# One core: the first loads and the order of every instruction found anew in a planned attention and channel-mix kernel

## The chip, the cores and the metric

The kernel runs on one core of one Trainium2 chip. The metric is the time of one execution on the device in microseconds (us), lower is better. The engines have these names in the profile: PE is TensorE's matmul, PEld its weight load, DVE is VectorE, ACT is ScalarE, POOL is GpSimd, SP is SyncE, which issues all the DMAs here.

## What is computed

Attention with rotary embeddings over 8 batches, 8 heads, 576 tokens and 64 dimensions a head; its output, 512 wide, goes through a gated channel mix with a hidden width of 1024. Everything is float32.

```
def _attn_ref(q, k, v):
    ...
    q_rot, k_rot = (rotate(q), rotate(k))
    scale = 1.0 / np.sqrt(D)
    scores = scale * np.matmul(q_rot, k_rot.transpose(0, 1, 3, 2))
    scores = scores - np.max(scores, axis=-1, keepdims=True)
    attn = np.exp(scores)
    attn = attn / (np.sum(attn, axis=-1, keepdims=True) + 1e-09)
    return np.matmul(attn, v).astype(np.float32)

def _moe_ref(x, mu_k, mu_r, w_k, w_v, w_r):
    ...
    xk = mu_k * x + (1.0 - mu_k) * x_prev
    xr = mu_r * x + (1.0 - mu_r) * x_prev
    k = np.maximum(xk @ w_k, 0.0)
    v = k * k @ w_v
    r = 1.0 / (1.0 + np.exp(-(xr @ w_r)))
    return (r * v).astype(np.float32)
```

## The kernel before

**Attention.** Two heads of a batch make a pair, and there are 32 pairs. For each pair `plan_rope` (L369) loads keys and queries with their swapped halves beside them (`xk`, `xq`, from one ring of two buffers, `nat`), multiplies both by the table of cosines and sines `turn`, and adds the two products. The first nine pairs (`PLAIN`) use the sum as it is (`kh`, `qh`); for the later ones it is split in a high and a low half (`kh`, `kl`, `qh`, `ql`), and the scores are made of three products. `plan_unit` (L429) makes the scores of 128 query rows: the products (L445), on VectorE the maximum (L454), on ScalarE the exponentials (L458), on VectorE the transposition of 32 x 32 blocks (L461). `plan_values` (L495) multiplies by the values in three parts (L520), and `plan_total` (L541) divides by the sums into `xT`.

**Channel mix.** `plan_mix` (L585) makes xk and xr of half a batch (288 tokens) and splits them (`mxh`, `mxl`). `plan_product` (L616) makes each product with the weights out of three (L625, L626, L627): high by high, low by high, high by low. `plan_key` (L635) makes relu, square and split (`kkh`, `kkl`), `plan_gate` (L666) the sigmoid, `plan_value` (L679) the product of both and the store.

**Weights.** They come in as raw 64-bit words, 20 blocks of 512 KB: 8 of w_k, 4 of w_r, 8 of w_v. `plan_convert` (L332) loads a block into a buffer of the ring `ql` (two buffers), decodes it with three steps on ScalarE (L345, L351) and two sums on VectorE or GpSimd (`wm`), casts it to the high half (L312 on ScalarE, L314 on VectorE) and subtracts for the low half.

**What sets the order.** No engine's order is written out. Each step is given to `Plan.op` with a rank, a list of what it needs, the buffers it uses and, for each engine that may do it, a duration and a bias. `Plan.issue` (L120) then plays the kernel through: an engine that becomes free takes, of the steps that are ready, the one with the lowest rank plus bias. The order so found is the order of the instructions of each engine. `one` and `two` (L294, L298) give a step to ScalarE or VectorE, and to GpSimd or VectorE; `B_SPLIT` is VectorE's bias for casts, `B_ROPE` for rotary steps, `B_LOW` for low halves. `lead` (L75) adds to a rank what `R` has for the kind of step and, for the first six pairs, what `EARLY` has. The rank of a pair is 18 times its number plus `PB`, that of a batch's channel mix 72 times its number plus `m0` and `MB`; a block of weights has a rank along `wk0` to `wk1` (or `wr`, `wv`) plus its entry in `WORDS`, and its load the same less 3. The load of keys and queries adds `ld`. All these numbers came out of a search. GpSimd and VectorE are played as taking turns for the steps marked with True (`port`), weighted by `WAIT`.

Of the kernel before, what the change touches and what calls it, by code (L numbers as in the profile page):

```python
# [25 lines left out]
R = dict(sg=146.09, k=35.07, q=51.6, v=-92.97, cs=-1440.03, ld=485.93, rope0=775.97, rope1=1341.24, rope2=-1593.82,
         split0=-490.14, split1=1651.45, u0=-9.23, u1=-9.99, u2=4.09, u3=-0.28, u4=-4.95, mx=-547.8, ex=-53.52,
         rz=-72.52, rs=-791.65, dg=-117.58, bd=451.61, tr=-238.29, ev=349.84, av=17.88, av2=630.69, tot=-1148.65,
         bor=-1152.78, m0=203.43, mh=-3.64, mk=10.46, mr=30.95, ms=1.47, tp=1238.89, rc=-454.17, mx1=-529.45,
         mx2=-1335.32, mx3=704.87, mg=3.37, mv=-0.23, dr=-1079.44, key0=1189.23, key1=-720.87, key2=14.38,  # L30
         gate0=-847.6, gate1=481.76, wk0=-48.7, wk1=233.61, wr0=-724.28, wr1=-1281.69, wv0=-20.84, wv1=1945.66)
# [4 lines left out]
EARLY = dict(k=(-1008.01, -482.85, -254.73, -397.74, 52.63, -212.54), q=(-618.65, -612.78, -339.46, -240.87, -281.62,  # L36
             23.47), v=(-438.31, -468.46, -152.53, -193.2, -99.8, -96.79), u0=(-1879.98, -368.38, -203.28, -241.45,
             75.91, 24.41), u1=(-217.97, -1062.91, -434.13, -122.46, 5.8, 24.25), u2=(-1055.68, -331.48, -170.26,
             -150.99, -114.87, 10.87), u3=(-1096.85, -646.9, -220.35, -256.66, -144.42, 32.2), u4=(-452.73, -641.08,
             -406.66, -274.78, 47.37, 35.29), mx=(-353.68, -484.47, -458.2, -302.05, -156.39, -150.07), ex=(-349.96,  # L40
             -41.28, -1342.06, 392.41, 2389.5, 993.44), tp=(-233.86, -2103.85, 654.43, -485.72, 608.35, 775.94),
             rs=(-93.75, 199.83, -142.38, -154.85, -142.68, -36.14), av=(14.66, -44.42, -95.87, -127.56, 58.88, 37.7),
             av2=(6.64, -352.36, -379.73, 83.33, -1292.92, 167.87), rc=(-1169.1, -848.81, -888.54, -532.26, -674.54,
             -118.59), tot=(-382.56, -430.1, -195.11, -8.86, -95.78, -89.47), rope0=(-853.79, -396.42, 1771.49, 997.6,
             520.07, -291.51), rope1=(-465.54, 808.19, -805.76, -1024.78, 647.78, -966.37), rope2=(-148.08, -152.31,
             -462.39, 3.34, -218.25, -248.75))
# [10 lines left out]


def act(n):
    return 0.833 * n + 100  # L60


def dve(n):
# [195 lines left out]
def rope_attention_channel_mix(ctx, tc, qt, kt, v, cs, mu, w_k, w_v, w_r, out):  # L259
# [4 lines left out]
    B, NP, _, _, S = kt.shape  # L264
# [38 lines left out]
    V, A, G, T = nc.vector, nc.scalar, nc.gpsimd, nc.tensor  # L303
# [28 lines left out]
    def plan_convert(t, src, hi, lo):  # L332
        d = {}
        s_w, s_e, s_m = Slot("ql"), Slot("kl"), Slot("wm")

        def load():
            words = sb.tile([P, 513, 2], U32, tag="ql", name="raw", bufs=BUFS["ql"])
            quarters = words.rearrange("p n w -> p (n w)").bitcast(I16)
            nc.sync.dma_start(quarters[:, 1:2049], src)
            d["middle"] = words[:, 0:512, 1]  # L340
            d["top"] = quarters.rearrange("p (n w) -> p n w", w=4)[:, 1:513, 0]

        def signed(n, tag, scale):
# [4 lines left out]
        e = op("A", t, act(512) + 130, lambda: signed("e", "kl", 1.0), [o], [s_w, s_e])  # L348
        m = op("A", t, act(512) + 130, lambda: signed("m", "wm", -1.0), [o], [s_w, s_m])
        m = op(two(512, B_LOW), t, 0, lambda e: combine(e, d["m"], d["e"], d["m"], ALU.subtract), [e, m], [s_m, s_e])  # L350
        e = op("A", t, act(512) + 80, lambda: A.mul(d["e"], d["middle"], 2.0 ** -13), [m], [s_w, s_e])  # L351
# [77 lines left out]
    def plan_unit(t, d, c):  # L429
# [17 lines left out]
        m = op("T", t, (8 if d["plain"] else 6) * (120 + 12), products, (d["q"][:c + 1] if d["plain"] else d["q"]) + d["k"], slots + d["sq"] + d["sk"], ("row" if c < 4 else "full", (8 if d["plain"] else 12) * len(heads)))  # L447
        for x in heads:
            s_m = Slot("nm")
            place = c + 5 * x  # L450
# [44 lines left out]
    def plan_values(t, d):  # L495
# [45 lines left out]
    def plan_total(t, d, half, w, slots, o, apart):  # L541
# [251 lines left out]
```

## Time and profile before

| | |
|---|---|
| median of 3 executions | 977.1 us (976.92 to 977.46) |
| the profiled execution | 977.65 us |
| its span, first to last instruction | 975.8 us |
| busy, share of the span | TensorE 94%, VectorE 79%, ScalarE 58%, GpSimd 54% |
| TensorE's mean granted clock | 0.983 |
| read from HBM, written | 88.74 MB, 9.44 MB |

The page of the profile gives each engine's busy time and count of instructions, then the span in 40 slices with a digit for the busy tenths of each. Matmuls are pipelined: a record is longer than the step from one to the next, and a TensorE that is shown as busy all the time may still have small gaps. A wait is put down to the last thing that released it.

### The profile page before, as it was taken

Reading aid. Unit: us, or ns where it says so; the run is one execution under the profiler, and the core shown is the slowest. Engines: PE = TensorE matmul, PEld = TensorE weight load, DVE = VectorE, ACT = ScalarE, POOL = GpSimd, SP = SyncE. Lnnn points to the kernel's source line nnn. Section 1 sums busy time; section 2 is a strip of 40 time slices with the busy share of each in tenths; the row PEclk is TensorE's granted clock in tenths of the full one; section 3 lists DMA queues with packets and bytes.
Section 4 is the critical chain, followed back from the end, with each engine's and each line's share of the span. In section 5 each row is a group of like instructions: output and inputs, shape, how many; then the busy total and the mean of one; then the engine's idle time right before and its main releaser. Section 6 shows DMA issues by size and latency. Waiting matters only on the chain.

```text
span 975.8 us, 34418 instructions
## 1 busy us (share of the span) xinstructions
PE 920.2 (94%) x15134; PEld 814.8 (83%) x15134; DVE 775.3 (79%) x1255; ACT 568.1 (58%) x1394; POOL 525.0 (54%) x551
## 2 busy tenths in 40 slices
PE   1888799999999999999999999999999999999998
PEld 1456588888989988899889998899888998989998
DVE  5999997986879878696896968797886969876552
ACT  4767885464747565474765747375664747544243
POOL 6988793543746556273753656474662647221201
PEclk9968899999999999999999999999999999999999
DMA  7455603422222333222233333033332232111000
GB/s 285 133 198 201 220 30 117 160 108 81 91 71 108 115 113 108 71 101 98 81 113 115 108 108 103 32 108 114 114 108 94 89 108 82 42 61 57 19 25 26
DMA packets 30854, 100.38 MB, mean 103 GB/s; under 512 B 3056, under 2 KB 11504, under 8 KB 26608
## 3 DMA queue, kind: packets, MB, share of 16 engines
q1 hardware_dynamic: 30704, 98.19, 28.8%
q8 instruction: 118, 1.93, 0.8%
q14 instruction: 32, 0.26, 0.1%
HBM read 88.74 MB, written 9.44 MB: 101 GB/s over the span
## 4 chain that ended last, share of the span: by engine, by line
PE 74%; DVE 18%; ACT 3%; DMA 2%; issue 2%; POOL 1%; SPq 0%; DVEq 0%; ACTq 0%
PE acc L625 18%; PE av L520 15%; PE acc L626 14%; PE acc L627 14%; PE s L445 12%; DVE nm L454 5%; DVE p L461 4%; DVE mxf L600 3%; DVE xk L308 2%; ACT p L458 2%; DMA xq<-in_qt 1%; DMA xk<-in_kt 1%; DVE rt L681 1%; PE av L526 1%; DVE xq L308 1%
## 5 line engine op out<-in xcount | busy, mean ns | idle before, releaser
L458 ACT ACTIVATE p<-s,nm 128x576 f32<-128x576 f32 x288 | 212.0, 740 | 99.6 <-DVE nm L454 98.5
L454 DVE TENSOR_REDUCE nm<-s 128x1 f32<-128x576 f32 x288 | 202.7, 737 | 13.4 <-PE s L445 12.9
L461 DVE STREAM_TRANSPOSE p<-p 128x576 f32<-128x576 f32 x288 | 206.7, 750 | 4.7 <-ACT p L458 4.6
L445 PE MATMUL s<-kh,qh 64*128 64x288 f32 (+1 forms) x738 | 143.8, 424 | 41.1 <-POOL qh L308 17.7
L520 PE MATMUL av<-p,values 32*64 32x144 f32 x9216 | 177.6, 293 | 2.7 <-issue 2.4
L520 PEld LDWEIGHTS av<-p,values 32*64 32x64 f32 x9216 | 150.9, 134 | 22.5 <-issue 19.4
L625 PE MATMUL acc<-mxh,wk_h 128*128 128x288 f32 x512 | 160.9, 314 | 3.4 <-ACT hr L642 3.2
L625 PE MATMUL acc<-kkh,wv_h 128*128 128x288 f32 x512 | 158.3, 309 | 4.5 <-DVE rt L681 4.3
L445 PEld LDWEIGHTS s<-kh,qh 64*128 64x128 f32 (+1 forms) x738 | 79.8, 204 | 88.6 <-ACT p L458 29.0
L626 PE MATMUL acc<-kkl,wv_h 128*128 128x288 f32 x512 | 151.1, 295 | 0.0
L626 PE MATMUL acc<-mxl,wk_h 128*128 128x288 f32 x512 | 150.8, 295 | 0.0
L627 PE MATMUL acc<-kkh,wv_l 128*128 128x288 f32 x512 | 150.8, 295 | 0.0
L627 PE MATMUL acc<-mxh,wk_l 128*128 128x288 f32 x512 | 150.6, 294 | 0.0
L308 POOL TENSOR_TENSOR kkl<-hr,kkh 128x288 fp32r<-128x288 f32 x97 | 88.1, 917 | 59.0 <-ACT kkh L312 42.1
L625 PEld LDWEIGHTS acc<-mxh,wk_h 128*128 128x128 f32 x512 | 96.1, 188 | 21.7 <-issue 14.1
L625 PEld LDWEIGHTS acc<-kkh,wv_h 128*128 128x128 f32 x512 | 96.1, 188 | 18.1 <-issue 11.1
L564 POOL COPY last<-xT 128x1 f32<-128x1 f32 x32 | 6.3, 196 | 190.3 <-DVE xT L557 190.3
L308 POOL TENSOR_TENSOR mxl<-mxf,mxh 128x288 fp32r<-128x288 f32 x77 | 69.7, 913 | 72.4 <-DVE mxh L314 49.4
L681 DVE TENSOR_TENSOR rt<-acc,rt 128x288 f32<-128x288 f32 x64 | 28.8, 449 | 95.3 <-PE acc L627 94.0
L548 ACT COPY rp<-av 128x288 f32<-128x288 f32 (+1 forms) x68 | 22.8, 389 | 135.3 <-PE av L526 134.8
L600 DVE SCALAR_TENSOR_TENSOR mxf<-xT,mu_t,mxf 128x288 f32<-128x288 f32 x128 | 95.6, 755 | 6.2 <-ACT mxf L595 5.2
L626 PEld LDWEIGHTS acc<-mxl,wk_h 128*128 128x128 f32 x512 | 96.3, 188 | 0.1
(85 smaller groups left out, 1945.2 us busy)
## 6 DMA issues: line engine op xcount, KB each, us to landing
values<-in_v SPq DMA_DIRECT2D x32, 1152.0 KB, 5.5
xq<-in_qt SPq DMA_DIRECT2D x31, 640.0 KB, 5.0
xk<-in_kt SPq DMA_DIRECT2D x32, 576.0 KB, 4.2
out_dram<-rt SPq DMA_DIRECT2D x64, 144.0 KB, 1.7
raw<-in_w_v SPq DMA_DIRECT2D x8, 512.0 KB, 4.1
raw<-in_w_k SPq DMA_DIRECT2D x8, 512.0 KB, 3.8
raw<-in_w_r SPq DMA_DIRECT2D x4, 512.0 KB, 5.5
turn<-in_cs SPq DMA_DIRECT2D x1, 640.0 KB, 4.9
```

Source lines behind the costliest of these rows:

```text
L308: (V if e == "V" else G).tensor_tensor(out=out, in0=a, in1=b, op=op)
L445: T.matmul(w[x][:, h, 0:H], lhsT=kind(d[q][r, c * P:(c + 1) * P]), rhs=kind(d[k][r, h * H:(h + 1) * H]), start=i == 0, stop=i == len(todo) ...
L454: V.tensor_reduce(out=w["nm", x], in_=w[x][:, :, 0:H], op=ALU.max, axis=AX.XY, negate=True)
L458: A.activation(out, w[x][:, :, 0:H].rearrange("p a (b n) -> p a b n", n=32), AF.Exp, bias=w["nm", x], scale=1.0, accum_out=d["sums"][:, pl ...
L461: V.transpose(queries(d, place), queries(d, place))
L520: T.matmul(at(a, x, 0), lhsT=d["vf"][g, b * P + x * D:b * P + x * D + D], rhs=d["pt"][g, b, x * Q:x * Q + Q], start=b == 0, stop=b == NB - 1)
L548: A.copy(w["r", half][:, i], r[..., 256:256 + N // 2])
L600: V.scalar_tensor_tensor(out=x["f"], in0=d["x", half][:, 1:1 + n], scalar=mu_t[:, m:m + 1], in1=x["f"], op0=ALU.mult, op1=ALU.add)
L625: T.matmul(w["a"], lhsT=w_h[:, i, sl], rhs=x["h"], start=(i == 0), stop=False)
L626: T.matmul(w["a"], lhsT=w_h[:, i, sl], rhs=x["l"], start=False, stop=False)
L627: T.matmul(w["a"], lhsT=w_l[:, i, sl], rhs=x["h"], start=False, stop=(i == count - 1))
L681: o = op("V", t + R["dr"], dve(n), lambda: V.tensor_tensor(out=x["r"], in0=w["a"], in1=x["r"], op=ALU.mult), [done, o], [s_a, s_r])
```

## The change

No step is added or taken away. The ranks (`R`, `PB`, `MB`, `EARLY`, `WORDS`), the biases and `WAIT` get other numbers, and eight durations that the planner plays with are set anew: a ScalarE step without its columns from 100 to 66 ns, the decoding steps, the exponentials (140 to 185 on top, so 720 to 731 ns in all), a unit of scores of plain pairs from 1056 to 936 and of later ones from 792 to 750, a block of the attention-value products from 268 to 245, the copy of the sums. By the new ranks the angles, the first keys and the first queries are asked for ahead of the first weights.

```
-R = dict(sg=146.09, k=35.07, q=51.6, v=-92.97, cs=-1440.03, ld=485.93, rope0=775.97, rope1=1341.24, rope2=-1593.82,
...
-         gate0=-847.6, gate1=481.76, wk0=-48.7, wk1=233.61, wr0=-724.28, wr1=-1281.69, wv0=-20.84, wv1=1945.66)
-PB = (-723.84, -349.44, -190.24, -77.24, -72.02, -34.42, -6.06, -3.63)
-B_COPY, B_ROPE, B_SPLIT, B_LOW, B_MIX, B_SQUARE, B_RELU, B_SMALL = 24.24, -108.4, -210.6, 1965.84, 1592.71, -340.79, 2795.13, 87.32
-MB = (-62.06, 30.2, 205.85, 245.13, 245.82, 267.52, 302.28, 1004.59)
+R = dict(sg=114.24, k=26.54, q=27.71, v=-165.25, cs=-2128.35, ld=527.56, rope0=639.18, rope1=1511.2, rope2=-2064.32,
...
+         gate0=-398.63, gate1=366.09, wk0=15.07, wk1=-105.67, wr0=-443.36, wr1=-1370.78, wv0=-8.87, wv1=1784.1)
+PB = (-668.25, -361.66, -199.7, -89.98, -84.16, -58.67, 7.84, 5.25)
+B_COPY, B_ROPE, B_SPLIT, B_LOW, B_MIX, B_SQUARE, B_RELU, B_SMALL = 24.24, 113.23, 75.44, 2514.79, 1178.12, -496.85, 2589.9, 87.32
+MB = (-48.78, 118.24, 163.28, 162.65, 217.96, 323.39, 533.17, 526.21)
...
-EARLY = dict(k=(-1008.01, -482.85, -254.73, -397.74, 52.63, -212.54), q=(-618.65, -612.78, -339.46, -240.87, -281.62,
...
+EARLY = dict(k=(-1894.6, -528.24, -282.01, -420.76, 120.85, -66.18), q=(-1780.54, -995.11, -351.98, -408.07, -163.76,
...
-WORDS = dict(wk=(-121.4, 190.81, -484.21, -187.48, -676.5, -230.26, -396.88, -48.1), wr=(-669.08, -168.07, -568.72,
-             -12.23), wv=(-1028.61, 127.34, -751.85, -1078.14, -297.95, -786.25, 273.13, -765.83))
+WORDS = dict(wk=(171.55, 485.05, -674.03, -560.38, -722.88, -154.92, -495.69, -447.27), wr=(14.78, -531.48, -610.94,
+             -55.56), wv=(-996.99, 319.78, -760.84, -1080.91, -32.96, -990.38, -21.43, -806.77))
...
-WAIT = 1.297e+06
+WAIT = 2.292e+04
...
 def act(n):
-    return 0.833 * n + 100
+    return 0.833 * n + 66
...
-        m = op("T", t, (8 if d["plain"] else 6) * (120 + 12), products, ...
+        m = op("T", t, ((936 if d["plain"] else 750) if c < 4 else (8 if d["plain"] else 6) * 132), products, ...
...
-            o = op("A", t + lead("ex", d["pi"]) + 0.1 * x, act(S) + 140, exponentials, [o], [slots[x], s_m, d["sp"], d["ss"]])
+            o = op("A", t + lead("ex", d["pi"]) + 0.1 * x, act(S) + 185, exponentials, [o], [slots[x], s_m, d["sp"], d["ss"]])
...
-            o = op("T", t + (i * lead("av2", d["pi"])), 2 * n * 134 + 2 * 134 * last, lambda i=i: part(i), ...
+            o = op("T", t + (i * lead("av2", d["pi"])), n * 245 + 244 * last, lambda i=i: part(i), ...
```

## Rows read from the trace of the kernel before

**Rows 1.** Three stretches: length; busy us and records of PE, PEld, DVE, ACT, POOL; clock, DMA.

```profile
0.00:10.40 10.40, 0.00 (x0) 0.00 (x0) 0.83 (x3) 5.96 (x8) 2.18 (x10) 1.00 0.83 293
10.40:117.60 107.20, 78.64 (x1384) 53.43 (x1384) 103.66 (x138) 74.01 (x158) 93.61 (x79) 0.84 0.57 201
117.60:972.60 855.00, 841.58 (x13751) 761.33 (x13750) 670.31 (x1114) 488.17 (x1230) 429.22 (x462) 1.00 0.26 88
```

**Rows 2.** Timeline of SyncE: start us, us, the load that it issues.

```profile
0.72 0.39 SPq L339 DMA_DIRECT2D raw<-in_w_r  x1
1.17 0.42 SPq L706 DMA_DIRECT2D turn<-in_cs  x1
...
2.58 0.65 SPq L378 DMA_DIRECT2D xk<-in_kt  x1
```

**Rows 3.** Timeline of the other engines at the start, idle time and releaser in brackets.

```profile
4.56 0.75 ACT L345 ACTIVATE we<-raw,below 128x512 int32<-128x512 int16 x1 [2.56 <-DMA raw<-in_w_r]
...
5.97 0.69 DVE L308 TENSOR_TENSOR wm<-we,wm 128x512 int32<-128x512 int32 x1 [5.13 <-ACT wm L345]
6.08 1.27 ACT L709 ACTIVATE turn<-turn 128x1280 f32<-128x1280 f32 x1
...
10.52 1.98 DVE L308 TENSOR_TENSOR xk<-xk,turn 128x576 f32<-128x576 f32 x1 [3.77 <-DMA xk<-in_kt]
...
17.75 3.24 PE L445 MATMUL s<-kh,qh 64*128 64x288 f32 x10 [17.75 <-POOL qh L308]
```

**Rows 4.** Loads, KB each, median us to landing: all key loads, then the angles.

```profile
xk<-in_kt SPq DMA_DIRECT2D x32, 576.0 KB, 4.2
...
turn<-in_cs SPq DMA_DIRECT2D x1, 640.0 KB, 4.9
```

**Rows 5.** By tile: ns min/median/max, first and last start in us.

```profile
L625 PE MATMUL acc<-mxh,wk_h x512: 289/295/509, 117.7 to 953.0; 128*128 128x288 f32 x171
...
L308 POOL TENSOR_TENSOR wv_l<-wm,wv_h x7: 1262/1299/1793, 35.0 to 144.6; 128x512 fp32r<-128x512 f32 x7
...
L625 PE MATMUL acc<-kkh,wv_h x512: 289/294/509, 150.2 to 972.0; 128*128 128x288 f32 x171
```

**Rows 6.** VectorE's groups from 10.4 to 117.6 us: busy us, mean ns, idle before.

```profile
L308 DVE TENSOR_TENSOR xk<-xk,turn 128x576 f32<-128x576 f32 x9 | 13.6, 1516 | 3.8 <-DMA xk<-in_kt 3.8
L308 DVE TENSOR_TENSOR xq<-xq,turn 128x640 f32<-128x640 f32 (+2 forms) x8 | 11.5, 1447 | 0.0
...
L314 DVE CAST wk_h<-wm 128x512 fp32r<-128x512 f32 x2 | 1.7, 835 | 0.2 <-POOL xT L562 0.2
...
L314 DVE CAST wr_h<-wm 128x512 fp32r<-128x512 f32 x1 | 1.4, 1399 | 0.0
L314 DVE CAST wv_h<-wm 128x512 fp32r<-128x512 f32 x1 | 1.3, 1274 | 0.0
```

**Rows 7.** By tile xk, whole span: ns min/median/max, first and last start.

```profile
L308 POOL TENSOR_TENSOR xk<-xk,turn x41: 1399/1430/1958, 10.5 to 813.1; 128x576 f32<-128x576 f32 x41
...
L308 DVE TENSOR_TENSOR xk<-xk,turn x23: 705/1131/1979, 10.5 to 815.1; 128x576 f32<-128x576 f32 x23
```

**Rows 8.** TensorE's waits from 250 to 880 us: total us, times, longest.

```profile
PE s L445 <- ACT p L458: 4.7, 6, 1.2
PE acc L625 <- DVE rt L681: 3.8, 4, 1.0
PE acc L625 <- ACT hr L642: 3.0, 5, 0.6
```

**Rows 9.** Chain that ended last, near 380 us: start us, us, what.

```profile
378.56 1.78 POOL ql L308
...
380.36 4.50 DMA xq<-in_qt
```

**Rows 10.** The same chain, an attention-value part; then its group on the page.

```profile
311.14 1.71 PE av L520 x96
...
L520 PE MATMUL av<-p,values 32*64 32x144 f32 x9216 | 177.6, 293 | 2.7 <-issue 2.4
```

More of the change, by code (lines that the diff above doesn't have):

```diff
@@ L25 @@
 PLAIN = 9
-R = dict(sg=146.09, k=35.07, q=51.6, v=-92.97, cs=-1440.03, ld=485.93, rope0=775.97, rope1=1341.24, rope2=-1593.82,
[L27 to L30, printed above, removed]
-         gate0=-847.6, gate1=481.76, wk0=-48.7, wk1=233.61, wr0=-724.28, wr1=-1281.69, wv0=-20.84, wv1=1945.66)
@@ L47 @@
-WORDS = dict(wk=(-121.4, 190.81, -484.21, -187.48, -676.5, -230.26, -396.88, -48.1), wr=(-669.08, -168.07, -568.72,
-             -12.23), wv=(-1028.61, 127.34, -751.85, -1078.14, -297.95, -786.25, 273.13, -765.83))
+R = dict(sg=114.24, k=26.54, q=27.71, v=-165.25, cs=-2128.35, ld=527.56, rope0=639.18, rope1=1511.2, rope2=-2064.32,
+         split0=-418.07, split1=1608.34, u0=-8.2, u1=-5.32, u2=1.49, u3=-6.02, u4=-0.73, mx=-544.32, ex=41.97,
+         rz=-695.55, rs=-754.16, dg=-117.58, bd=451.61, tr=-238.29, ev=349.84, av=13.51, av2=784.94, tot=-1475.95,
+         bor=-1328.95, m0=291.99, mh=-0.32, mk=-23.68, mr=-5.73, ms=2.69, tp=1071.62, rc=-270.84, mx1=-892.1,
+         mx2=-1659.22, mx3=643.01, mg=3.82, mv=0.3, dr=-1319.74, key0=1331.92, key1=-528.48, key2=397.69,
+         gate0=-398.63, gate1=366.09, wk0=15.07, wk1=-105.67, wr0=-443.36, wr1=-1370.78, wv0=-8.87, wv1=1784.1)
@@ new lines @@
+PB = (-668.25, -361.66, -199.7, -89.98, -84.16, -58.67, 7.84, 5.25)
+B_COPY, B_ROPE, B_SPLIT, B_LOW, B_MIX, B_SQUARE, B_RELU, B_SMALL = 24.24, 113.23, 75.44, 2514.79, 1178.12, -496.85, 2589.9, 87.32
+MB = (-48.78, 118.24, 163.28, 162.65, 217.96, 323.39, 533.17, 526.21)
+NE = 6
+EARLY = dict(k=(-1894.6, -528.24, -282.01, -420.76, 120.85, -66.18), q=(-1780.54, -995.11, -351.98, -408.07, -163.76,
+             20.68), v=(-313.84, -466.2, -566.04, -215.27, -126.88, 68.8), u0=(-2315.28, -271.51, -448.14, -301.33,
+             -109.73, -63.6), u1=(-386.55, -870.03, -323.12, -142.79, -62.19, 14.61), u2=(-875.18, -508.09, -196.7,
+             -230.87, -55.43, -50.21), u3=(-1377.19, -764.16, -201.77, -112.33, -132.29, -25.44), u4=(-531.2, -525.98,
+             -407.08, -247.46, -52.6, -80.53), mx=(-632.72, -629.35, -442.49, -448.34, -385.52, -228.35), ex=(-610.02,
+             111.8, -1480.22, 597.82, 2474.47, 797.93), tp=(362.2, -2650.19, 484.55, -96.23, 633.48, 504.81),
+             rs=(133.33, -184.35, -175.83, -175.58, -65.69, 59.18), av=(-148.5, -76.89, -113.79, -116.09, 35.62,
+             5.99), av2=(250.66, -554.68, -325.83, 446.76, -1656.68, -132.39), rc=(-1009.01, -644.13, -615.36,
+             -628.04, -651.4, -278.2), tot=(-887.51, -629.27, -171.89, -250.51, -148.73, -127.64), rope0=(-739.43,
+             -550.11, 1901.03, 1063.51, 499.47, -78.05), rope1=(-896.71, 188.81, -210.14, -1415.44, 601.97, -980.71),
+             rope2=(-134.4, -231.6, 131.18, 273.47, -60.6, -101.5))
@@ L347, in plan_convert @@
         o = dma(t - 3, P * 4096, load, [], [s_w])
-        e = op("A", t, act(512) + 130, lambda: signed("e", "kl", 1.0), [o], [s_w, s_e])
-        m = op("A", t, act(512) + 130, lambda: signed("m", "wm", -1.0), [o], [s_w, s_m])
+        e = op("A", t, act(512) + 99, lambda: signed("e", "kl", 1.0), [o], [s_w, s_e])
+        m = op("A", t, act(512) + 99, lambda: signed("m", "wm", -1.0), [o], [s_w, s_m])
         m = op(two(512, B_LOW), t, 0, lambda e: combine(e, d["m"], d["e"], d["m"], ALU.subtract), [e, m], [s_m, s_e])
-        e = op("A", t, act(512) + 80, lambda: A.mul(d["e"], d["middle"], 2.0 ** -13), [m], [s_w, s_e])
+        e = op("A", t, act(512) + 11, lambda: A.mul(d["e"], d["middle"], 2.0 ** -13), [m], [s_w, s_e])
         m = op("G", t, pool(512), lambda: combine("G", d["m"], d["m"], d["e"], ALU.add), [m, e], [s_m, s_e])
@@ L445, in products @@
                         T.matmul(w[x][:, h, 0:H], lhsT=kind(d[q][r, c * P:(c + 1) * P]), rhs=kind(d[k][r, h * H:(h + 1) * H]), start=i == 0, stop=i == len(todo) - 1)
-        m = op("T", t, (8 if d["plain"] else 6) * (120 + 12), products, (d["q"][:c + 1] if d["plain"] else d["q"]) + d["k"], slots + d["sq"] + d["sk"], ("row" if c < 4 else "full", (8 if d["plain"] else 12) * len(heads)))
+        m = op("T", t, ((936 if d["plain"] else 750) if c < 4 else (8 if d["plain"] else 6) * 132), products, (d["q"][:c + 1] if d["plain"] else d["q"]) + d["k"], slots + d["sq"] + d["sk"], ("row" if c < 4 else "full", (8 if d["plain"] else 12) * len(heads)))
         for x in heads:
@@ L535, in plan_values @@
             need = need + [d["R"]] if last else need
-            o = op("T", t + (i * lead("av2", d["pi"])), 2 * n * 134 + 2 * 134 * last, lambda i=i: part(i), need, slots + [d["sp"], d["sv"]] + [d["srw"]] * last, ("row", 32 * (n + last)))
+            o = op("T", t + (i * lead("av2", d["pi"])), n * 245 + 244 * last, lambda i=i: part(i), need, slots + [d["sp"], d["sv"]] + [d["srw"]] * last, ("row", 32 * (n + last)))
             need = [o]
@@ L566, in border @@
                 G.tensor_copy(xT[:, 0:1], d["last"])
-        o = op("A", t + lead("rc", d["pi"]) + 0.1 * half, act(288) + 60 + 160 * apart, copied, [o], slots + [s_r])
+        o = op("A", t + lead("rc", d["pi"]) + 0.1 * half, act(288) + 160 * apart, copied, [o], slots + [s_r])
         o = op("V", t + lead("tot", d["pi"]) + 0.1 * half, dve(288) + 30 + 130 * apart, total, [o], slots + [s_r, sx])
```

10 lines of the change are left out of this document (removed).

## Prediction

> **What bounds the kernel now.** I read the page first: TensorE is busy for 94% of the span and VectorE for 79%, but TensorE's slices differ between the first few and the rest, so these are averages over stages. I cut the span where the first feed-forward product starts, at 117.7 us [rows 5], and where the first key lands, and asked for the busy time in three stretches [rows 1]. Until 10.4 us the loads set the pace: TensorE does nothing, VectorE is busy for 0.83 us. From 10.4 to 117.6 us VectorE is busy for 103.66 of 107.2 us (97%), GpSimd for 93.61, ScalarE for 74.01; TensorE is granted a clock of 0.84 on average and still waits, so its half-speed stretches cost nothing there. From 117.6 to 972.6 us TensorE is busy for 841.58 of 855 us. So the time is three pieces added up: a start of 10.4 us that waits for data, a prologue of 107 us set by VectorE and by what it shares with GpSimd, and 855 us set by TensorE. The last 3.2 us (975.8 − 972.6) are the last store.
>
> **The sum's base.** The profiled execution took 977.65 us, 1.85 us more than its span of 975.8, and 0.55 us (0.06%) more than the median of 977.1. A gain read in the trace I take off the median.
>
> **Part 1: the first loads.** No instruction is added or taken away; the planner's ranks change, and with them every engine's order. The ranks of the first loads can be added up by hand. Before: the third block of w_r has −724.28 − 278.70 − 568.72 − 3 = −1574.7, the angles −1440.0, the first block of w_r −1396.4, the first keys −723.84 + 35.07 − 1008.01 + 485.93 = −1210.9, the first queries −805.0. That is the order of SyncE in the trace: raw at 0.72 us, turn at 1.17, then mu and a second raw, xk at 2.58 [rows 2]. After: angles −2128.4, keys −668.25 + 26.54 − 1894.6 + 527.56 = −2008.8, queries −1893.5 and −1779.3, and only then w_r with −443.36 − 463.71 − 610.94 − 3 = −1521.0. All of them go through SyncE's one queue; what moves back in it are two blocks of w_r, and whoever waits for those moves back too: ScalarE's first decoding step, and behind it GpSimd's first sum.
>
> What it is worth: VectorE's first rotary multiplication starts at 10.52 us, after 3.77 us of waiting for the keys [rows 3]. The keys are the fifth load issued, and 512 + 640 + 4 + 512 KB stand ahead of them. Afterwards only 640 + 4 KB do. The nearest row is the angles' own in the kernel before: second in the queue behind 512 KB, issued at 1.17 us, landed 4.9 us later, at 6.1 us [rows 2, 4]. The keys would be issued at about 1.6 us; with 4.2 us to landing (the median of all key loads, [rows 4]) they are there at 5.8 us, with 4.9 us at 6.5 us. ScalarE's scaling of the angles (1.27 us, [rows 3]) ends by then if the angles land at about 4.7 us as the first raw block did (ScalarE took it up at 4.56 us, [rows 3]). I take 6.5 us, 4.0 us earlier than 10.52. But VectorE had already done 0.69 us of weight work in that time [rows 3], and GpSimd at most the 2.18 us for which it was busy at all [rows 1]; this must now be done later. VectorE's net is 3.3 us, GpSimd's 1.8 or more. **I take −3.0 us**, nearer to VectorE's, which is the fuller, between −4.7 (5.8 us, nothing moved behind) and 0 (the first rival). The first product, at 17.75 us before [rows 3], should move further, to 11 to 13 us: from the first rotary step it took 7.2 us (17.75 − 10.52), in which GpSimd's weight steps stood between the rotary steps. That further gain counts for nothing, since TensorE waits for VectorE through the whole prologue.
>
> **Part 2: who does the shared steps.** An operation that several engines can do is taken by the engine that first reaches it; a bias makes VectorE take it later. For casts to the high half (B_SPLIT) that goes from −210.6 to +75.4, for rotary steps (B_ROPE) from −108.4 to +113.2. VectorE should give up casts to ScalarE, and rotary steps to GpSimd. In the prologue VectorE did four casts of weights, 1.4 + 2 × 0.835 + 1.3 = 4.4 us [rows 6]; ScalarE has 107.2 − 74.0 = 33 us to spare. If all go, the prologue is 4.4 us shorter; if none, nothing. **I take −2.0 us**, about half, since ScalarE is also the engine that the exponentials wait on.
>
> The rotary steps are harder. VectorE does 9 + 8 of the multiplications in the prologue, at some 1.5 us each [rows 6]. A key multiplication takes it 0.705 us at best, 1.131 in the middle and 1.979 at worst, while GpSimd's takes 1.40 to 1.43 [rows 7]: the long ones stand beside a GpSimd step. If eight moved, VectorE would be free of 8 × 1.5 = 12 us by the rows' durations, but GpSimd, which has only 107.2 − 93.6 = 13.6 us left, would get 8 × 1.43 = 11.4. If the two engines take turns in truth, each step moved costs 1.43 − 0.70 = 0.73 us more, +5.8 us for eight. **I take 0**, between −5.6 (VectorE's own work in eight steps, 8 × 0.70 us, leaves and GpSimd takes it in its idle time) and +5.8. The Trainium skill, in "SBUF — State Buffer", section "Who interferes with whom", says that a VectorE instruction with two SBUF inputs and a GpSimd instruction that reads SBUF exclude each other for the whole instruction. By it the +5.8 us would hold and the forecast would be some 975.5 us. That the key multiplication's 0.705 us become 1.979 [rows 7] agrees with it, as far as one line can show.
>
> **Part 3: the 855 us.** Of these TensorE's visible waits are few: between 250 and 880 us 4.7 + 3.8 + 3.0 = 11.5 us [rows 8], in fifteen pieces of 1.2 us at most, about 2 us in each batch (eight batches share the 855 us, 107 us each, and 630 us hold 5.9 of them). One place shows how a wait comes about: GpSimd's kl and ql release the buffer, and only then the next queries can be loaded, which takes 4.50 us [rows 9]. The planner's durations are now closer to the rows: a third of the attention-value products (96 records) spans 1.71 us, and 0.29 us of that is the length of its last record [rows 10], so it takes 1.4 to 1.5 of TensorE's time; the planner had 6 × 268 = 1608 ns and gets 6 × 245 = 1470. With the old figure it thought TensorE later than it is, by 138 ns for each of 96 thirds, and placed the steps that free PSUM accordingly. An order for the right durations may close some of these waits. All closed gives −11.5 us, doubled +11.5. **I take −2.5 us**, a fifth of them: the same buffers and the same four engines stay.
>
> **Sum:** −3.0 − 2.0 + 0 − 2.5 = −7.5 us; 977.1 − 7.5 = 969.6, which I give as **970.0 us**.
>
> **The rivals.** *Weights too late, no change: 977 us.* The conversion of the weights starts about 4.5 us later. For it: w_v's last low half was started at 144.6 us and its high half first multiplied at 150.2 us [rows 5], 5.6 us of slack, little more than the delay. Against it: VectorE and GpSimd are ahead by nearly as much by then. If the slack is gone the 5 us of parts 1 and 2 come back as TensorE waiting near 150 us, 974.5 to 978.
>
> *More than I count: 960 us.* Parts 1 and 2 at their bounds (4.7 + 4.4) and most of the waits closed (8 of 11.5): 977.1 − 17.1 = 960, with a span of 957 to 965. For it speaks that VectorE is at 97% in the prologue, so whatever it gives away counts in full; against it that GpSimd is at 87%.
>
> *Slower: 983 us.* Rotary steps that go to GpSimd lengthen the chain of buffers in each batch: ql (1.78 us) stands on GpSimd ahead of the next load [rows 9], and a rotary step queued in front of it costs 1.43 us [rows 7] or more. TensorE now loses about 2 us in a batch. One step of 1.6 us more (between the 1.43 and the 1.78) in each of seven batches is 11.2 us, less the 5.0 of parts 1 and 2: +6.2 us. It decides against the change from 5.0 / 7 = 0.7 us a batch on. For it speaks the shift of B_ROPE; against it that GpSimd is busy for only 429 of the 855 us [rows 1], so that most steps would find it free.
>
> *That the loads don't move* I rule out: the ranks reproduce the queue of before.
>
> **How the numbers follow.** Forecast 966 to 974: 0.48. Weights too late: 0.20. More: 0.15. Slower: 0.17. About 0.2% (2 us) is what a measurement of this kernel can tell from no change. Faster by more: 0.48 + 0.15 + a quarter of "weights too late" (0.05) = 0.68; within: 0.13; slower: 0.17 + 0.02 = 0.19. The range leaves out the lower third of "more" (0.05) and the upper part of "slower" (0.11): 960 to 981. Its upper end takes in part 3's +11.5 less 7.5.
>
> **What would show it.** Right: the keys' multiplication on VectorE starts at 6 to 7 us; the first product at 11 to 13; the first feed-forward product at 112 to 113.5 instead of 117.7; no VectorE casts of weights in the prologue; TensorE's waits of 250 to 880 us at about 9. Wrong: a first feed-forward product at 116 or later (the head was given back), a wait of TensorE for weights near 150 us, or more than 18 us of waits in the steady part. I am wrong by most if the prologue's length follows GpSimd rather than VectorE.

## The result: 961.0 us, by an order in which TensorE hardly pauses

| | before | after |
|---|---|---|
| median of four executions (lowest to highest) | 977.0 us (976.5 to 977.5) | 961.0 us (959.0 to 963.5) |
| profiled execution, its span | 977.65, 975.8 | 959.55, 957.8 |
| VectorE's first rotary step starts at | 10.52 | 7.38 |
| first score product | 17.75 | 13.47 |
| first feed-forward product | 117.7 | 114.7 |
| from there to the last product's start | 854.6 | 838.9 |
| one batch, mean of four | 113.2 | 110.2 |

After over before is 0.9838 (95%: 0.981 to 0.9866). The forecast was 970, its range 960 to 981: the sign and the range held, but the gain is 16 us where 7 were forecast. Of the 18.1 us between the two spans (975.85 and 957.77) 2.95 lie ahead of the first feed-forward product and 15.8 between it and the last product; behind that, the last store gives 0.6 back. "One batch" is the time from the 129th to the 385th product of `kkh` by `wv_h`, divided by four: 379.86 to 832.76 us before, 372.01 to 812.70 after.

The same three stretches as [rows 1], now of the kernel after (length; busy us and records of PE, PEld, DVE, ACT, POOL; clock, DMA):

```profile
0.00:7.40 7.40, 0.00 (x0) 0.00 (x0) 0.25 (x3) 2.55 (x2) 0.91 (x9) 1.00 0.72 231
7.40:114.70 107.30, 74.84 (x1376) 50.88 (x1377) 103.16 (x139) 78.66 (x164) 95.66 (x79) 0.84 0.59 209
114.70:953.90 839.20, 838.39 (x13758) 761.89 (x13758) 666.02 (x1110) 490.03 (x1233) 426.48 (x464) 1.00 0.26 91
```

The start is 3 us shorter, the prologue as long as it was (107.3 against 107.2 us), and in the long stage TensorE is busy for 838.39 of 839.2 us, where it was busy for 841.58 of 855. The granted clocks are the same, stretch by stretch.

The start of after, timelines of four engines merged (start us, us, engine and line, idle time and releaser in brackets):

```profile
0.72 0.39 SPq L706 DMA_DIRECT2D turn<-in_cs  x1
...
1.64 0.65 SPq L378 DMA_DIRECT2D xk<-in_kt  x1
...
3.62 1.35 SPq L339 DMA_DIRECT2D raw<-in_w_r  x2
...
4.67 1.27 ACT L709 ACTIVATE turn<-turn 128x1280 f32<-128x1280 f32 x1 [2.67 <-DMA turn<-in_cs]
...
7.38 0.76 DVE L308 TENSOR_TENSOR xk<-xk,turn 128x576 f32<-128x576 f32 x1 [2.35 <-DMA xk<-in_kt]
...
13.47 0.85 PE L445 MATMUL s<-kh,qh 64*128 64x288 f32 x2 [13.47 <-DVE qh L308]
```

The loads go out in the order that the ranks gave [rows 2]; the keys are there 5.7 us after their issue (7.38 − 1.64).

TensorE's waits between 250 and 880 us, of which before had 4.7 + 3.8 + 3.0 [rows 8], are gone: the same view of after lists none. What three of them were can be seen in before. Timelines merged; first TensorE and ScalarE near 360 us, then all four engines from 386 to 395 us:

```profile
359.40 0.74 ACT L458 ACTIVATE p<-s,nm 128x576 f32<-128x576 f32 x1 [0.95 <-DVE nm L454]
359.70 0.29 PE L627 MATMUL acc<-mxh,wk_l 128*128 128x288 f32 x1
360.14 0.40 ACT L642 ACTIVATE hr<-acc 128x288 f32<-128x288 f32 x1
360.59 0.40 PE L625 MATMUL acc<-mxh,wk_h 128*128 128x288 f32 x1 [0.60 <-ACT hr L642]
...
386.02 2.08 POOL L308 TENSOR_TENSOR xq<-xq,turn 128x640 f32<-128x640 f32 x1
386.60 1.81 DVE L600 SCALAR_TENSOR_TENSOR mxf<-xT,mu_t,mxf 128x288 f32<-128x288 f32 x1
388.33 1.41 DVE L454 TENSOR_REDUCE nm<-s 128x1 f32<-128x576 f32 x2
388.66 0.39 PE L445 MATMUL s<-kh,qh 64*128 64x288 f32 x1
389.11 0.74 ACT L458 ACTIVATE p<-s,nm 128x576 f32<-128x576 f32 x1 [2.48 <-DVE nm L454]
389.64 1.55 POOL L308 TENSOR_TENSOR xq<-xq,turn 128x640 f32<-128x640 f32 x1
389.66 1.84 DVE L600 SCALAR_TENSOR_TENSOR mxf<-xT,mu_t,mxf 128x288 f32<-128x288 f32 x1
390.00 0.40 PE L445 MATMUL s<-kh,qh 64*128 64x288 f32 x2 [0.94 <-ACT p L458]
...
393.35 0.29 PE L627 MATMUL acc<-kkh,wv_l 128*128 128x288 f32 x1
394.09 0.44 DVE L681 TENSOR_TENSOR rt<-acc,rt 128x288 f32<-128x288 f32 x1
394.58 0.40 PE L625 MATMUL acc<-kkh,wv_h 128*128 128x288 f32 x1 [0.93 <-DVE rt L681]
```

Three pauses, which come again in each of the four batches from 380 to 833 us:
- (a) At 359.70 TensorE needs an accumulator that the relu (L642) frees. The relu stands on ScalarE behind an exponential that itself waited 0.95 us for its maximum.
- (b) At 388.66 TensorE needs the place of scores that the exponential of 389.11 frees. That one waited 2.48 us for its maximum, which on VectorE stood behind a mixing step (L600) of 1.81 us. Beside it runs a rotary step on GpSimd.
- (c) At 393.35 TensorE needs the accumulator that `rt` (L681) frees, and `rt` comes late on the same VectorE, behind the second mixing step, 1.84 us long beside the next rotary step, and two transpositions and two maxima that follow it.

Measured from one product's start to the next, where 0.13 us is usual between feed-forward products (and taken for the scores of (b) too), they cost 0.89, 1.34 and 1.23 us, so 0.76 + 1.21 + 1.10 = 3.07 us a batch: the whole difference of 113.2 and 110.2. As waits the view lists 0.60 + 0.94 + 0.93 = 2.47 us of them, since it counts only from the end of a record of 0.29 to 0.39 us.

### The profile page after: what moved, and what is told of

Its sections match the earlier page's. It is cut to its first block, busy times and chain, and to the rows that moved or that the text cites. A ratio compares the mean times of both kernels' runs of the same rounds, so it can differ in the third digit from the quotient of the medians.

```text
span 957.8 us, 34401 instructions
## 1 busy us (share of the span) xinstructions
PE 913.2 (95%) x15134; PEld 812.8 (85%) x15134; DVE 769.9 (80%) x1251; ACT 571.2 (60%) x1398; POOL 523.0 (55%) x551
## 4 chain that ended last, share of the span: by engine, by line
PE 85%; DVE 10%; issue 2%; DMA 1%; ACT 1%; POOL 0%; SPq 0%; DVEq 0%
PE acc L625 20%; PE acc L626 16%; PE acc L627 16%; PE av L520 16%; PE s L445 15%; DVE nm L454 2%; DVE p L461 2%; DVE mxf L600 1%; DMA xk<-in_kt 1%; DVE xq L308 1%; DVE xk L308 1%; PE av L526 1%; ACT p L458 1%; DVE kh L308 0%; DVE xT L557 0%
## 5 line engine op out<-in xcount | busy, mean ns | idle before, releaser
L461 DVE STREAM_TRANSPOSE p<-p 128x576 f32<-128x576 f32 x288 | 210.0, 754 | 9.9 <-ACT p L458 9.8
L445 PE MATMUL s<-kh,qh 64*128 64x288 f32 (+1 forms) x738 | 141.0, 419 | 36.7 <-DVE qh L308 13.5
L308 POOL TENSOR_TENSOR mxl<-mxf,mxh 128x288 fp32r<-128x288 f32 x72 | 64.1, 893 | 99.4 <-DVE mxh L314 78.3
L626 PEld LDWEIGHTS acc<-kkl,wv_h 128*128 128x128 f32 x512 | 96.3, 188 | 0.1
L627 PEld LDWEIGHTS acc<-kkh,wv_l 128*128 128x128 f32 x512 | 96.3, 188 | 0.0
L627 PEld LDWEIGHTS acc<-mxh,wk_l 128*128 128x128 f32 x512 | 96.3, 188 | 0.0
L600 DVE SCALAR_TENSOR_TENSOR mxf<-xT,mu_t,mxf 128x288 f32<-128x288 f32 x128 | 90.7, 719 | 4.6 <-ACT mxf L595 3.2
```

The costliest lines, as they stand in the source:

```text
L308: (V if e == "V" else G).tensor_tensor(out=out, in0=a, in1=b, op=op)
L600: V.scalar_tensor_tensor(out=x["f"], in0=d["x", half][:, 1:1 + n], scalar=mu_t[:, m:m + 1], in1=x["f"], op0=ALU.mult, op1=ALU.add)
L626: T.matmul(w["a"], lhsT=w_h[:, i, sl], rhs=x["l"], start=False, stop=False)
L627: T.matmul(w["a"], lhsT=w_l[:, i, sl], rhs=x["h"], start=False, stop=(i == count - 1))
```

## The experiments

There are two kinds of edit. In e1 to e4 ranks or durations of the two kernels are mixed, and the planner finds an order anew. In e5 to e12 its order is kept as a list of (step, engine), the steps are issued along that list, and at most named steps are moved in it, so that nothing else changes.

### The loads alone, and the loads taken back

`e1_loads_first`, the kernel before with the three ranks that bring angles, keys and queries ahead:

```diff
-cs=-1440.03, ... EARLY = dict(k=(-1008.01, ... q=(-618.65, ...
+cs=-2128.35, ... EARLY = dict(k=(-1894.6, ... q=(-1780.54, ...
```

> The kernel before with three ranks alone from the change: the angles (cs), the first pair's keys and the first pair's queries; so angles, keys and queries are loaded ahead of the first weights, and everything else keeps its rank, bias and duration. My theory: the changed kernel's first feed-forward product came 3.0 us earlier (114.7 against 117.7 us), and that is the loads' part alone; so this kernel is 3 us faster, 974 us, and its steady part keeps its three waits a batch (about 13 us of visible TensorE waits behind 117 us). Rival: the early start lets every later step fall differently, and the steady part's waits go with it: 962 to 966 us. Second rival: the weights that come later eat the start: 977 us.

Measured: 980.7 us, 1.0034 of before (1.0021 to 1.0047). By tile, starts of the first and last product:

```profile
L625 PE MATMUL acc<-mxh,wk_h x512: 289/295/514, 119.2 to 956.0; 128*128 128x288 f32 x171
```

The first score product came at 13.44 us, 4.3 earlier than before, and the first feed-forward product at 119.2 instead of 117.7: 1.5 us *later*. Before's own start, the same list in four profiled executions (before, e5, e7, e9), puts that product at 117.0 to 117.9. The same early start, in an order that was not found for it, is worth less than nothing.

`e6_loads_by_hand`, the order of before kept, with only the start re-ordered:

```diff
+first = [0, 2, 7, 12, 17, 2017, 1999, 22, ...]   # angles, mu, keys, queries, queries, w_r, w_r, values, ...
+return [(i, engine[i]) for i in first] + [x for x in order if x[0] not in first]
```

> The kernel before with the order of every engine as it is, but for the start: SyncE asks for angles, keys and first queries ahead of the two weight blocks, and the four steps of the first weight block stand behind the first rotary steps on ScalarE, VectorE and GpSimd, as in the changed kernel. No rank is touched, so nothing later is ordered anew. Theory of part 1 of the prediction: the first rotary step at 7.4 us instead of 10.5, the first feed-forward product about 3 us earlier (114.7 us), 974 us. Rival: weights that come 5 us later leave VectorE and GpSimd waiting within the next 20 us, and the first feed-forward product stays at 117 to 118 us, 977 us (with the loads' three ranks alone it came at 119.2).

Measured: 978.8 us, 1.0018 (1.0009 to 1.0028). Its timeline of VectorE, and its first feed-forward product:

```profile
7.92 0.76 DVE L308 TENSOR_TENSOR xk<-xk,turn 128x576 f32<-128x576 f32 x1 [2.78 <-DMA xk<-in_kt]
...
20.92 1.99 DVE L308 TENSOR_TENSOR wm<-we,wm 128x512 int32<-128x512 int32 x1 [6.42 <-POOL wm L308]
```

```profile
L625 PE MATMUL acc<-mxh,wk_h x512: 289/295/510, 118.9 to 953.1; 128*128 128x288 f32 x171
```

VectorE starts 2.6 us earlier and then idles 6.42 us, because the next step in its order needs a weight sum that GpSimd makes late: the head start is lost to the weights that were put back. `e8_both_by_hand` puts this start and the moves of e5 (below) into one kernel.

> The two edits by hand together, on the order of the kernel before: the steps moved in each batch, and the loads first with the start shifted. If the changed kernel's gain is these two things and no more, this is 961 us like it (13 + 3 off 977); if either is given back, it shows here as in its own run, 964 to 977 us.

Measured: 970.8 us (0.9936, 0.9921 to 0.9951), 2.7 us more than those moves alone (968.1, below): the start by hand costs there as well.

The other direction. `e4_after_weights_first` is the kernel after with the three load ranks of before; `e11_after_loads_back` keeps after's order on every engine and turns only SyncE's first eight loads back:

```diff
+first = [2017, 0, 2, 2008, 7, 12, 22, 17]   # w_r, angles, mu, w_r, keys, queries, values, queries
+return [(i, "S") for i in first] + [x for x in order if x[0] not in first]
```

> The changed kernel with three ranks put back: angles, first keys and first queries, so that a weight block is again loaded ahead of the angles and two ahead of the keys. Theory: only the start is undone, first product near 17 to 18 us, first feed-forward product near 117.7 us, steady part without waits as in the changed kernel: 964 us. Rival (the steady order hangs on the start): waits come back behind 117 us, 970 us or more.

> The changed kernel in its own order on every engine but SyncE, where the first eight loads go back to the order of the kernel before (a block of w_r, angles, mu, a second block of w_r, keys, queries, values, queries). Theory: in an order made for early keys their four us count almost in full, since VectorE starts its rotary steps at 10.5 instead of 7.4 us and has no weight step to put ahead: first feed-forward product at 117.5 to 118.5 instead of 114.7, 964 to 965 us. Rival: the head is made up later by what VectorE has to spare, 961 us within 1. A third: engines that can't take another step while they wait lose more than the 3.1 us, 967 us or more.

Measured: 984.1 us (1.0081 of before, 1.006 to 1.0102) and 966.3 us (0.9883, 0.9859 to 0.9907). The same row of the two, the first e4's:

```profile
L625 PE MATMUL acc<-mxh,wk_h x512: 289/295/510, 128.0 to 958.0; 128*128 128x288 f32 x171
```

```profile
L625 PE MATMUL acc<-mxh,wk_h x512: 289/296/511, 118.1 to 937.8; 128*128 128x288 f32 x171
```

In after's own order the late keys cost 2.3 to 3.4 us at the first feed-forward product (118.1 against 115.8 and 114.7 in two profiled executions of after's order), about what they gained; by the medians 966.3 − 960.6 = 5.7 us, with intervals of both that allow some 2 to 9. Of the three expectations the first (964 to 965) is nearest to the profiled 963.2, and the median lies between it and the third. When the planner finds the order anew for the old load ranks (e4), it loses 13 us ahead of the first feed-forward product and 11 more between the first and the 129th product of `kkh` by `wv_h` (162.1 to 396.2 us, so 234.2, where after takes 223.4). Only then do its batches take 110.2 us each, as after's. TensorE's listed waits from 128 to 400 us are 6.8 us. So the rival of this run (waits come back) held up to about 396 us, its first theory (no waits) behind that: the steady batches don't hang on the load ranks, the order up to them does.

### Ranks and durations apart

`e2_durations` has the ranks of before and the eight new durations; `e3_ranks` the ranks of after and the old durations.

> The kernel before with all its ranks, biases and loads, and the planner's durations alone set as in the change (a ScalarE step 34 ns shorter, the exponentials 11 ns longer, a unit of scores and a third of the attention-value products 6 to 12% shorter). Theory that the durations do it: the same ranks played with the right times give an order without the three waits a batch, some 13 to 16 us less, 961 to 964 us. Theory that the newly found ranks do it: these ranks fit the old durations, so the waits stay or get others, 974 to 985 us.

> The changed kernel with all its ranks, biases and loads, and the planner's durations put back to those of the kernel before. Theory that the durations do it: the ranks alone keep only the 3 us of the loads, 972 to 976 us, and waits of TensorE come back in each batch. Theory that the newly found ranks do it: 961 to 965 us and next to no waits of TensorE behind 117 us.

Measured: 1012.7 us (1.0369, 1.0353 to 1.0385) and 999.1 us (1.0223, 1.0207 to 1.0238). A batch takes 118.7 and 117.5 us. TensorE's waits from 250 to 880 us of the first, its largest rows, then the largest of the second:

```profile
PE s L445 <- ACT p L458: 11.8, 13, 2.2
PE av L520 <- ACT p L458: 5.8, 5, 1.3
PE acc L625 <- ACT hr L642: 3.2, 5, 1.1
```

```profile
PE av L520 <- ACT p L458: 9.4, 9, 2.0
```

Each half of the change alone makes the kernel 22 to 36 us slower. Durations nearer to the trace are no gain by themselves: the ranks hold only for the durations that they were found with.

### The pauses, one cause at a time

`e5_waits_by_hand`: the order of before, in which VectorE makes two maxima ahead of a mixing step and `rt` ahead of two maxima in four batches, and ScalarE the relu ahead of the exponential in five. `before_op` puts the steps that it is given ahead of the last one named; `done` are the products that `rt` needs.

```diff
+for k in range(4):
+    order = before_op(plan, order, maxima[126 + 36 * k:128 + 36 * k], mixed[45 + 16 * k])
...
+    order = before_op(plan, order, done + value[17 + 8 * k:18 + 8 * k], maxima[128 + 36 * k])
+for k in range(5):
+    order = before_op(plan, order, relu[22 + 12 * k:23 + 12 * k], exps[119 + 36 * k])
```

> The kernel before with the order of every engine as it is (same loads, same engine for every step), but for a handful of steps moved by hand where TensorE waits in each batch: on VectorE a pair of maxima goes ahead of the mixing step (mxf) that it stands behind, and a gate product (rt) ahead of the pair of maxima in front of it, in four batches; on ScalarE a relu that frees TensorE's accumulator goes ahead of an exponential that waits for VectorE, in five batches. Theory A, the order at three places of a batch makes the waits: the three pauses (0.90, 1.33 and 1.23 us from one product's start to the next) go, 4 x (1.33 + 1.23 - 0.26) + 5 x (0.90 - 0.13) = 13.0 us, 964 us. Theory B, VectorE is late there by the amount of its work: what is moved ahead pushes the rest back, and the pauses come up a few us later, 972 to 977 us.

Measured: 968.1 us, 0.9904 (0.9888 to 0.9921), −8.7 us. Thirteen moves in a list of 4795 steps bring half of the change's gain. Its waits from 250 to 880 us:

```profile
PE s L445 <- ACT p L458: 3.3, 10, 0.5
```

Pause (a) is gone in all five places; (b) and (c) have become one of two pieces, 0.55 and 0.72 us from start to start at 392.1 us and once in each batch after. A batch takes 111.0 us. So the pauses are real and the order has a part in all three, but one of the two mixing steps there is still 1.68 us long (the first is back at 0.50), and VectorE is late for somebody.

`e7_short_rotary` takes the suspected cause away: the order of before, but GpSimd's rotary multiplications and sums cover 32 columns from the tenth pair on, and the other columns of these steps are left out.

```diff
+c1 = c0 + 32 if e == "G" and not plain else c1
...
-lambda e: combine(e, m["c"], m["c"], m["s"], ALU.add)
+lambda e: combine(e, *(m[z][:, 0:32 if e == "G" else w] for z in "ccs"), ALU.add)
```

> The kernel before with the order of every engine as it is; GpSimd's rotary multiplications and sums are done on 32 columns instead of 576 or 640 from the tenth pair on, and the rest of these columns is left out. That takes away most of the time for which GpSimd holds what it shares with VectorE there (a mixing step takes VectorE 1.8 us beside a GpSimd rotary step and 0.5 us alone). Theory C, the waits come from these collisions: VectorE is on time at 388 and 393 us, two of the three pauses a batch go (4 x 2.3 = 9 us), the third shrinks, 965 to 968 us. Theory A (the order alone): VectorE's mixing steps get shorter but the pauses stay at half or more, 972 to 976 us.

Measured: 965.3 us, 0.9878 (0.9863 to 0.9893), −11.6 us. Waits from 250 to 880 us, to be set beside [rows 8]:

```profile
PE acc L625 <- ACT hr L642: 3.0, 5, 0.6
PE s L445 <- ACT p L458: 0.4, 1, 0.4
```

(b) and (c) are gone, (a) stands unchanged, five times, 3.0 us. VectorE's groups in the same stretch, two of before and then the same two of this kernel (busy us, mean ns of one):

```profile
L454 DVE TENSOR_REDUCE nm<-s 128x1 f32<-128x576 f32 x200 | 140.8, 737 | 11.6 <-PE s L445 11.2
L600 DVE SCALAR_TENSOR_TENSOR mxf<-xT,mu_t,mxf 128x288 f32<-128x288 f32 x89 | 69.7, 789 | 3.2 <-ACT mxf L595 2.7
```

```profile
L454 DVE TENSOR_REDUCE nm<-s 128x1 f32<-128x576 f32 x202 | 142.3, 738 | 12.1 <-PE s L445 11.7
L600 DVE SCALAR_TENSOR_TENSOR mxf<-xT,mu_t,mxf 128x288 f32<-128x288 f32 x92 | 61.1, 673 | 3.7 <-ACT mxf L595 2.7
```

At the place of (b) and (c), which lies near 385 us in this kernel, its timeline of VectorE has the two mixing steps that took 1.81 and 1.84 us:

```profile
383.95 0.51 DVE L600 SCALAR_TENSOR_TENSOR mxf<-xT,mu_t,mxf 128x288 f32<-128x288 f32 x1
...
385.71 0.50 DVE L600 SCALAR_TENSOR_TENSOR mxf<-xT,mu_t,mxf 128x288 f32<-128x288 f32 x1
```

So the mixing steps shorten (789 to 673 ns in the mean), the maxima, which read one input, from PSUM, take 737 and 738 ns whatever GpSimd does. Thus (b) and (c) come from the collision of a VectorE step with two inputs from SBUF and a GpSimd step, and (a) has nothing to do with it. A rotary step on GpSimd is not what TensorE waits for; it stretches the step on VectorE that stands ahead of the maximum.

`e9_relu_short` joins this with the five moves of the relu; `e10_after_short` shortens the rotary steps in the order of after; `e12_after_frozen` is after itself, replayed, on the same chip.

> The kernel before in its own order, with two edits together: in five batches the relu that frees an accumulator stands ahead of the exponential on ScalarE, and GpSimd's rotary multiplications and sums cover 32 columns from the tenth pair on (the other columns of these steps are left out). Theory: three pauses a batch make up the gain of the 855 us stage, two of them from VectorE's collisions with GpSimd's rotary steps, one from ScalarE's order, and they add up: 965.3 us (short rotary steps alone) less 5 x 0.9 = 4.5 us, 960.8 us, with the stage from the first feed-forward product at 842.2 - 4.5 = 837.7 us and no pause over 0.8 us between 340 and 820 us. Rival: what one pause hides comes out when it goes, as in the run with waits moved by hand (8.7 of 13.0 us came): a new pause of 0.5 us or more each batch and 963 to 965 us.

> The changed kernel in its own order, with GpSimd's rotary multiplications and sums on 32 columns from the tenth pair on (the rest of these steps left out). Theory: the new order already keeps the steps that TensorE waits for away from these collisions, so taking GpSimd's part off gives little: between 959 and 961 us, at most the pause of 0.45 us that is left once a batch (4 x 0.45 = 1.8 us). Rival: the collisions still cost in the new order and its gain came from elsewhere: 4 us or more below the changed kernel, 957 us or less.

> The changed kernel itself with its order of instructions replayed from a list instead of found anew: the base for the two runs beside it on the same chip. Every theory expects 959 to 963.5 us, the times that the changed kernel showed; whether its times lie closer together here than those 4.5 us is open.

Measured: 963.5 us (0.9856, 0.9841 to 0.9871), 961.6 us (0.9845, 0.9818 to 0.9872) and 960.6 us (0.9831, 0.9808 to 0.9854); before was 977.6 on that chip. With both causes removed the order of before takes 110.1 us a batch, as after's does, and 839.8 us from the first feed-forward product to the last, where after takes 838.9. The total of 963.5 is above the 960.8 expected, though no new pause of 0.5 us a batch came in. Some 1.0 us of the difference lies ahead of the stage, where e7 and this kernel have the same list and the first feed-forward product came at 117.0 and 117.9. In the stage the moves of the relu brought 0.56 us a batch (110.63, e7, to 110.07) where 0.9 had been counted. (a) costs only 0.76 above the usual step, and the other 0.2 come back in pieces too small to name. So the rival's time came, not by its route. From 380 to 833 us, four batches, after gains 12.2 us on before and this kernel 12.6: there the three pauses are the whole of it. Between the first product of `wv_h` and 380 us after gains 6.3 us more, this kernel 1.7. Most of these other 4.6 us are given back elsewhere: after makes 3758 products in this stretch and before 3781, and the parts of the stage ahead of it and behind the four batches take after 1.4 and 1.3 us longer than before (this kernel 0.9 less and 0.4 more). Over the whole stage after gains 15.8 us and this kernel, before's order without its pauses, 14.8; what the last 1.0 is was not taken apart.

In after's order shorter rotary steps change nothing that can be measured (961.6 against 960.6). The windows of e10 and of e12 from the first feed-forward product on:

```profile
115.40:954.60 839.20, 838.19 (x13758) 761.86 (x13758) 645.63 (x1110) 489.08 (x1233) 288.01 (x464) 1.00 0.27 91
```

```profile
115.80:955.70 839.90, 838.91 (x13758) 762.03 (x13758) 666.35 (x1110) 490.07 (x1233) 425.80 (x464) 1.00 0.27 91
```

138 us of GpSimd's work and 21 of VectorE's are gone, and the stage is 0.7 us shorter. The collisions are still there in after; they hit nothing that TensorE waits for. Its timeline near 414 us shows one place, GpSimd and VectorE merged:

```profile
411.93 1.43 POOL L308 TENSOR_TENSOR xk<-xk,turn 128x576 f32<-128x576 f32 x1
412.85 1.12 DVE L308 TENSOR_TENSOR xk<-xk,turn 128x576 f32<-128x576 f32 x1
413.30 2.10 POOL L308 TENSOR_TENSOR xq<-xq,turn 128x640 f32<-128x640 f32 x1
413.89 1.41 DVE L454 TENSOR_REDUCE nm<-s 128x1 f32<-128x576 f32 x2
415.22 2.16 DVE L461 STREAM_TRANSPOSE p<-p 128x576 f32<-128x576 f32 x3
415.36 1.42 POOL L308 TENSOR_TENSOR xk<-xk 128x576 f32<-128x576 f32 x1
```

While GpSimd turns keys and queries, VectorE makes maxima and transpositions, which take their usual 0.7 us each.

## Why the prediction was right in direction and too small

**Part 1, −3.0 us: right in amount, wrong in reason.** The first feed-forward product came 2.95 us earlier (117.66 to 114.71; by the other profiled executions of the same two lists 1.2 to 3.2). But the sum let the early keys bring this by themselves. The runs show that they bring nothing alone (119.2 and 118.9 in e1 and e6): the first rival, that weights come too late, is what happens when only the loads move, as the 6.42 us of e6 show; in e1, where the whole order was found anew, the cause was not traced. The gain needs a prologue found for it, and there the loads are worth about what was counted (e11: 2.3 to 3.4 us at that product). The marks: the keys' multiplication was put at 6 to 7 us, and came at 7.38, since the third load landed 5.7 us after its issue and not 4.9, the time of the angles [rows 4]; the first product at 13.47 just missed 11 to 13; 114.7 missed 112 to 113.5, by the 2 us of part 2 that did not come.

**Part 2, −2.0 us: nothing.** The bias was read as a move of casts away from VectorE, and half of their 4.4 us [rows 6] as gain. First a row of before's prologue that belongs beside [rows 6] (10.4 to 117.6 us), then VectorE's groups in the prologue of after (7.4 to 114.7 us):

```profile
L308 DVE TENSOR_TENSOR wm<-we,wm 128x512 int32<-128x512 int32 x4 | 4.3, 1066 | 0.0
```

```profile
L308 DVE TENSOR_TENSOR xk<-xk,turn 128x576 f32<-128x576 f32 x8 | 11.1, 1390 | 2.4 <-DMA xk<-in_kt 2.4
L308 DVE TENSOR_TENSOR xq<-xq,turn 128x640 f32<-128x640 f32 x7 | 11.1, 1593 | 0.0
L308 DVE TENSOR_TENSOR wm<-we,wm 128x512 int32<-128x512 int32 x6 | 7.2, 1202 | 0.1
...
L314 DVE CAST wv_h<-wm 128x512 fp32r<-128x512 f32 x2 | 1.8, 904 | 0.0
...
L314 DVE CAST wr_h<-wm 128x512 fp32r<-128x512 f32 x2 | 1.0, 518 | 0.0
```

Four casts of weights are still there, 2.8 us instead of 4.4, and the decoding sums went from four of 4.3 us to six of 7.2. What one kind of step gave up another took: VectorE is busy for 103.16 of 107.3 us, as before for 103.66 of 107.2. The planner gives an engine the next ready step, and so fills what a bias frees; the mistake was to count one kind of work without what would move into its place. The rotary multiplications in the prologue, nine and eight before, are eight and nine now: the value of 0 held, but by luck, since it was the middle of two costs of a move that did not happen. The bias had been read as sending them to GpSimd; over the whole span the key multiplications went the other way:

```profile
L308 POOL TENSOR_TENSOR xk<-xk,turn x37: 1402/1432/1946, 7.5 to 794.0; 128x576 f32<-128x576 f32 x37
...
L308 DVE TENSOR_TENSOR xk<-xk,turn x27: 732/881/2021, 7.4 to 795.3; 128x576 f32<-128x576 f32 x27
```

41 and 23 they were [rows 7]. With this falls the rival "slower", whose one condition was that these steps move to GpSimd. The 975.5 us that the port's rule would have given (975.4 by the prediction's own terms) went with it, since it rested on eight steps going to GpSimd. The rule itself, of the Trainium skill, "SBUF — State Buffer", section "Who interferes with whom", is borne out where it had not been looked for: mixing steps of two SBUF inputs took 1.81 and 1.84 us beside GpSimd's rotary steps and 0.52 us in the median of the whole span, and one that began beside a rotary step ended 0.3 us after it (386.02 + 2.08 and 386.60 + 1.81). That is 0.2 us less than its own record of 0.5 us, so the records show the two excluding each other for most of the instruction and not for the whole of it.

**Part 3, −2.5 us: the step that failed, a term mis-sized; 15.8 us measured.** The waits were the right place [rows 8] and their mechanism, an order that frees PSUM late, was the right one. Two readings made the term small. First, "a fifth of them, since the same buffers and the same four engines stay" was no reason: e5 closes 2.2 of a batch's 3.1 us (113.2 to 111.0) by moving four steps in it, with the same buffers, engines and durations. Thirteen of the fifteen waits are three pauses that recur, (a) five times, (b) and (c) four times each; the other two are waits for a place of scores near 276 and 281 us. What removed such a pause in one batch removed it in each (e5 for (a), e7 for (b) and (c)). Second, the 11.5 us were too few: 2.47 us of listed waits in a batch were 3.07 from start to start, by which 11.5 are some 14. The sum spread them over batches of 107 us, an eighth of the stage, as "about 2 us in each"; a batch takes 113.2. What was not asked was the question that e7 answers: who makes the releaser late. The row names VectorE's `rt` or ScalarE's `p`; further back on VectorE stands a mixing step of 1.8 us beside GpSimd. The chain that was read instead (`ql`, the next queries, [rows 9]) does lead to VectorE just ahead of (b), at 384.9 us. But VectorE had no idle time there, GpSimd took the queries up at 386.02, 1.2 us after they had landed, and e5 and e7 close or shrink the pauses with SyncE's order as it was. And the durations, to which the part gave the credit, make the kernel slower without ranks to match (e2).

**The rivals.** "More than I count, 960" had the time (961.0) and its span of 957 to 965, by another route: it took parts 1 and 2 at their bounds, 9.1 us, and 8 of the waits; in truth the two gave 3.0 and the stage 15.8. "Weights too late" holds for the loads by themselves, and in after no wait for weights shows. That half of the chance lay on 966 to 974 goes back to the fifth.

## What to carry to other kernels

Where one engine is busy for 98% of a stage, list its waits by their place in the repeating unit, not by their total: here a pause that recurred at one place had the same cause each time, and moving one relu in each batch removed (a) everywhere. Follow each back beyond the releaser to what delayed the releaser on its own engine; here that was a neighbour ahead of it on the same engine that waited for something else, or a step stretched more than threefold by another engine. Ranks and modelled durations are one setting: here either without the other cost 22 to 36 us.

## What the runs showed of the hardware that had not been expected

One list of instructions has times several us apart. After and its replay took 959.0 to 963.9 us in eight executions, e10 959.5 to 964.4, e11 963.2 to 968.6, all with after's list (e11 but for eight loads); e5, e7 and e9, with before's list (but for the moves named), stayed within 1.4 us each (967.0 to 968.4, 964.5 to 965.8, 962.7 to 964.1), before itself, measured anew beside each set of runs, within 2.5 us in three sets and 4.5 us in the fourth (976.0 to 980.6). In the two profiled executions of after's list (959.55 and 961.38 us) the first feed-forward product stands 1.1 us apart (114.71 and 115.80) and the stage behind it 0.7 (838.88 and 839.59). What in the prologue differs from one execution to the next stays open.
